# A gated mix of memory attention and a SwiGLU network on one core: attention visits by quads of heads, with shorter holds of PSUM banks

## The chip, the cores and the metric

The kernel runs on one core of one Trainium2 chip. Its engines are TensorE (PE, with PEld for its weight loads), VectorE (DVE), ScalarE (ACT), GpSimd (POOL) and SyncE (SP, which only issues transfers). The metric is the device time of one launch in microseconds. The kernel before took 1145.44 us as the median of three runs, which lay between 1144.23 and 1146.28.

## The reference

Input `x` has 2048 rows of 640 features. Two branches are computed from it and mixed by a gate per row.

```python
x = A_x                                     # [1, 2048, 640]
g = _sigmoid((x * gate_w).sum(-1, keepdims=True))
a = _A_ref(x, A_wq, A_wk, A_wv, A_wo, A_beta)
b = _B_ref(x, B_w1, B_w3, B_w2)             # (silu(x w1) * (x w3)) w2, 1728 hidden features
return g * a + (1 - g) * b

# _A_ref: 32 heads of 20 features, 4 segments of 512 rows
for s in range(N):
    qs, ks, vs = q[:, :, s], k[:, :, s], v[:, :, s]
    logits = jnp.einsum("bhqd,bhkd->bhqk", qs, ks) * scale + mask
    p = _softmax(logits, axis=-1)
    a_dot = jnp.einsum("bhqk,bhkd->bhqd", p, vs)
    pq = phi(qs)                            # where(t > 0, t + 1, exp(t))
    num = jnp.einsum("bhld,bhde->bhle", pq, M)
    den = jnp.einsum("bhld,bhd->bhl", pq, z)[..., None] + 1e-6
    o = g * num / den + (1.0 - g) * a_dot
    outs.append(o)
    pk = phi(ks)
    M = M + jnp.einsum("bhld,bhle->bhde", pk, vs)
    z = z + jnp.einsum("bhld->bhd", pk)
```

## The kernel before

**Numbers in two parts.** Each fp32 operand of the large products is held as a rounded part and a remainder, and a product is three matmuls (`PASSES`). `split` (L112) makes the parts: ScalarE casts (L113), GpSimd or VectorE subtracts (L114).

**Work beside attention.** The segments are handled as two groups, A (0 and 1) and B (2 and 3). For each group come the projections Q, K and V (`q_block`, `k_block`, `v_blocks`), the memory (`memory_turn`, `memory_write`), the reads of memory (`memory_read`, segments 1 to 3), the network (`ffn_up`, `ffn_down`) and the output projection (`oproj`). Each is a generator that yields after a few hundred nanoseconds of matmul work, with an estimate of it.

**Weights.** `w_load` (L155) issues the load of the next weight into one of two raw buffers, on SP. Items 0 and 1 are weights of Q, 2 to 6 those of V, 7 to 11 those of K, 12 the next of Q. `w_split` makes the two parts in one of six `W` tiles. A load waits until the raw buffer's last subtract is done.

**Attention.** A head has three units of logits. `s_unit` computes logits with queries as rows (L564), and VectorE takes the row maxima (L572, an addition of the mask with a running maximum). `max_rows` (L576) rounds the 8 columns of maxima of a pair of heads (L580), takes the remainder (L581) and turns 32 x 32 blocks (L584); transfers from GpSimd's queue (L587) put them as extra rows beside Q, so that `t_unit` (L589) gets transposed logits with the maximum already subtracted (L600). ScalarE takes exp into `P` (L605), GpSimd zeroes above the diagonal (L613). `pv_quad` (L618) multiplies P by V for four heads (L624); the values come in `vg` tiles for eight heads.

**The order.** TensorE's order is the program's. `attention` (L711) counts slots; a pair of heads has 20. At slots 5 and 15 a visit is made: the units of pair t's logits, of pair t-2's transposed logits, and every second pair P V. The loop at the end of `gated_mix` runs the other generators between visits, and before a visit steps up to four times until the group of matmuls in progress has reached `READY` (800). The other engines' orders come from a scheduler with estimated times, apart from what is pinned by `here` or `behind`.

**PSUM.** There are eight banks. `bank_tile` (L118) takes them in rotation. A projection or network group holds its bank out of the rotation until it is filled. `parts` (L274) empties a Q or K group: copy, exp, minimum with 1 (L282), remainder (L283), maximum with 0 plus the exp (L285).

```python
VISITS = {5: ((0, 1), (0,)), 15: ((2,), (1, 2))}      # slot: units of logits, units of P
P32 = sp.tile([P, 1280], F32, tag="P32", bufs=4)      # one per head
```

Of the kernel before, what the change touches and what calls it, by code (L numbers as in the profile page):

```python
# [27 lines left out]
RH, READY = 3 * DH, 800  # L28
NP, AGE = 4, 4
# [8 lines left out]
def gated_mix(ctx: ExitStack, tc: tile.TileContext, xT, wqk, wv, w13, w2, w2h, wo, beta, out):  # L38
# [15 lines left out]
    qk = [cp.tile([P, 2, L], FR, name=f"qk{i}") for i in range(NST)]  # L54
    gH = cp.tile([P, H], F32, name="gH")
# [10 lines left out]
    def constants():  # L66
# [4 lines left out]
        for i in range(2):  # L71
            nc.gpsimd.memset(nsT[i].bitcast(F32), 0.0)
# [45 lines left out]
    def bank_tile(name, hold=False):  # L118


        k = free.pop(0)
        ps = pp.tile([P, L], F32, tag=f"b{k}", name=name, bufs=1)
        if hold:
            held[k] = 0
        else:
            free.append(k)
        return ps

    def filled():

        (k, _), = held.items()
        held.clear()
        free.append(k)
# [19 lines left out]
    raws, clock = [], dict(step=0, oldest=0, next=0)  # L153

    def w_load():  # L155
        k = clock["next"]
        src, n = items[k]
        if k in EARLY:
            raw = sp.tile([P, 1280], F32, tag="P32", name=f"wr{k}", bufs=NP)
        else:  # L160
            raw = sp.tile([P, D + 2], F32, tag="wraw", name=f"wr{k}", bufs=NRAW)
        nc.sync.dma_start(raw[:, :n], src)
# [111 lines left out]
    def parts(name, ps, phi=None):  # L274
# [4 lines left out]
        if phi is not None:  # L279
            e = f_tile("phi_t")  # L280
            last["act"] = nc.scalar.activation(e, ps, AF.Exp)
            nc.vector.tensor_scalar(e, e, 1.0, None, op0=ALU.min)  # L282
        nc.vector.tensor_sub(s[:, 1], ps, s[:, 0].bitcast(F32))  # L283
        if phi is not None:
            nc.vector.scalar_tensor_tensor(phi, ps, 0.0, e, op0=ALU.max, op1=ALU.add)  # L285
# [19 lines left out]
    def q_block(c, mb, i, alloc, oldest=None):  # L305
        ps = bank_tile(f"q{c}_{mb}", True)
# [8 lines left out]
    def memory_read(c):  # L315
        pq = big.pop(("q", c))[:, :KB * L].rearrange("p (b n) -> p b n", b=KB)
        for qb in range(4):
            gm = ht_tile([P, D], F32, f"gm{c}_{qb}")
            for hf in range(2):
# [8 lines left out]
                for n, (b, a0, u0, u1) in enumerate(todo):  # L328
# [3 lines left out]
                                     start=n == 0, stop=n == len(todo) - 1, skip_group_check=True)  # L332
                r = sp.tile([P, 16], F32, tag="r16", name="nd_r")
# [9 lines left out]
    def v_blocks(c, iv, end):  # L343
# [7 lines left out]
        for lb in range(4):  # L351
# [5 lines left out]
            for hf in range(2):  # L357
                n0, n1 = (0, 320) if hf == 0 else (320, 642)
                ps = bank_tile(f"v{c}_{lb}_{hf}", True)
# [20 lines left out]
    def k_block(c, mb, i, prev):  # L380
# [3 lines left out]
        ps = bank_tile(f"k{c}_{mb}", True)  # L384
# [85 lines left out]
    def ffn_up(cs, j, idx, oldest=None):  # L470
        half = j == NF
        for c in cs:
            ws = [w_get(i, idx[0] if oldest is None else oldest) for i in idx]
            x = Xs[c]
            pg = bank_tile(f"g{c}_{j}", True)
# [5 lines left out]
            if not half:  # L481
# [5 lines left out]
                pu = bank_tile(f"u{c}_{j}", True)  # L487
# [3 lines left out]
            else:  # L491
# [5 lines left out]
                nc.gpsimd.tensor_sub(ht[64:, 0], t[:64], ht[:64, 0].bitcast(F32))  # L497
            yield 699

    def ffn_down(cs, js, idx, last=False):  # L500
        first = js[0] == 0
        w2s = [w_get(i, idx[0]) for i in idx]
        for c in cs:
            if first:
                accs[c] = slot(f"acc{c}")[:, :4 * D].rearrange("p (b d) -> p b d", b=4)
            for lb in range(4):
                for hf in range(2):
                    ps = bank_tile(f"f{c}_{js[0]}_{lb}_{hf}", True)
# [22 lines left out]
    def load_pair(p):  # L531
# [9 lines left out]
        if h % 8 == 0:  # L541
            v = sp.tile([P, 4, VG + 12], F32, tag="vg", name=f"vg{j}", bufs=NVG)
            nc.gpsimd.memset(v[:, :, VG:], 0.0)
            i = nc.sync.dma_start(v[:, :, :VG], vd[c][:, :, VE * h:VE * h + VG])
            if j < 8:
                here(i)
            bank["v"] = v
        m = sp.tile([P, 8], F32, tag="m", name=f"m{j}", bufs=4)
# [3 lines left out]
        pairs[p] = dict(t=t, m=m)  # L552
# [457 lines left out]
```

## Time and profile before

| | |
|---|---|
| Median of three runs | 1145.44 us |
| The profiled execution | 1145.62 us |
| Its span in the profile | 1143.9 us |
| Mean granted clock of TensorE | 0.997 |
| Busy: PE, DVE, POOL, ACT | 1125.0, 651.0, 558.7, 449.7 us |
| Bytes moved | 152.05 MB, mean 133 GB/s |

The largest groups of matmuls are those of the network (L251 `g` and `u`, 216.8 and 202.3 us; L514 `f`, 204.0 us). Of attention's groups, L564 and L624 have 76.3 and 75.5 us. VectorE's largest group is the row maxima, 250.8 us; GpSimd's is the subtract of weight parts, 197.6 us.

How to read it: a line of the timeline gives the start, the time, the engine and line, the operation with its tiles and shape, and in brackets how long the engine was idle before it and what ended that. A group of lines gives busy time and mean nanoseconds of one. A window gives its length and then each engine's busy time in it. An issue of a transfer (SPq, POOLq, ACTq) is not counted as busy.

### The profile page before, as it was taken

What the parts mean: (1) busy time and instruction counts of PE and PEld (TensorE: products, weight loads), DVE (VectorE), ACT (ScalarE), POOL (GpSimd) and SP (SyncE); (2) the same over time, 40 slices, a digit from 0 to 9 for tenths busy, and PEclk for the clock granted to TensorE, in tenths of its full rate; (3) what the DMA queues carried; (4) which work ended last, traced back from release to release, by engine and by line L of the source; (5) the groups of instructions that cost most, each with busy time, mean ns of one, the idle gap of its engine ahead of it and who ended that gap; (6) DMA issues with size and microseconds to landing.
All of it is one profiled execution on the core that took longest, in us unless ns stands there. A gap on an engine that the chain in (4) does not pass through costs nothing.

```text
span 1143.9 us, 19984 instructions
## 1 busy us (share of the span) xinstructions
PE 1125.0 (98%) x6953; PEld 904.9 (79%) x6953; DVE 651.0 (57%) x1987; ACT 449.7 (39%) x884; POOL 558.7 (49%) x811
## 2 busy tenths in 40 slices
PE   9989999999999999999999989999999999999998
PEld 6978877877877897878977766868778787877888
DVE  5033475555655653565345788775666776662534
ACT  5244234544343333253444534435543344344140
POOL 5053355555555346365354445664764457454150
PEclk9999999999999999999999999999999999999999
DMA  8275733324434225325386765363534324342112
GB/s 323 91 226 196 246 105 91 98 79 122 107 98 115 66 74 157 104 73 178 108 271 228 267 185 138 97 183 110 176 104 108 100 69 138 91 132 64 48 58 93
DMA packets 84725, 152.05 MB, mean 133 GB/s; under 512 B 19728, under 2 KB 29456, under 8 KB 84624
## 3 DMA queue, kind: packets, MB, share of 16 engines
q1 hardware_dynamic: 55632, 98.29, 26.2%
q0 software_dynamic: 22080, 38.58, 13.8%
q10 hardware_dynamic: 6912, 13.90, 3.3%
q8 instruction: 56, 0.92, 0.3%
q14 instruction: 45, 0.37, 0.1%
HBM read 95.25 MB, written 54.53 MB: 131 GB/s over the span
## 4 chain that ended last, share of the span: by engine, by line
PE 87%; issue 4%; DVE 3%; DMA 3%; POOL 1%; ACT 1%; SPq 0%; POOLq 0%; ACTq 0%; DVEq 0%
PE f L514 17%; PE g L251 17%; PE u L251 16%; PE o L624 6%; PE q L251 6%; PE s L564 5%; PE v L363 4%; PE k L251 4%; PE op L765 4%; PE t L600 3%; DMA wr<-in_wqk_dram 1%; PE pm L417 1%; PE nd L329 1%; DVE junk L572 1%; POOL W L114 1%
## 5 line engine op out<-in xcount | busy, mean ns | idle before, releaser
L572 DVE CUSTOM_DVE_ANT_0 junk<-s,mask 128x128 bf16<-128x128 f32 (+3 forms) x512 | 250.8, 490 | 153.9 <-PE s L564 117.5
L114 POOL TENSOR_TENSOR W<-wr,W 128x640 fp32r<-128x640 f32 (+1 forms) x126 | 197.6, 1574 | 253.6 <-ACT W L113 201.5
L605 ACT ACTIVATE P<-t 128x384 f32<-128x384 f32 (+1 forms) x384 | 174.7, 530 | 280.9 <-PE t L600 165.5
L251 PE MATMUL g<-X,W 128*128 128x512 f32 x840 | 216.8, 401 | 1.4 <-DVE ns L581 1.4
L514 PE MATMUL f<-W,ht 128*128 128x320 f32 x1312 | 204.0, 313 | 1.7 <-DVE m L572 1.2
L251 PE MATMUL u<-X,W 128*128 128x512 f32 x780 | 202.3, 401 | 0.0
L514 PEld LDWEIGHTS f<-W,ht 128*128 128x128 f32 x1312 | 194.5, 189 | 8.8 <-issue 2.6
L251 PEld LDWEIGHTS g<-X,W 128*128 128x128 f32 x840 | 153.4, 188 | 40.9 <-issue 7.2
L613 POOL TENSOR_SCALAR_AFFINE_SELECT P<-P 128x256 f32<-128x256 f32 x256 | 98.4, 416 | 159.4 <-ACT P L605 159.4
L251 PEld LDWEIGHTS u<-X,W 128*128 128x128 f32 x780 | 142.8, 188 | 36.7 <-issue 3.7
L113 ACT CAST W<-wr 128x640 fp32r<-128x640 f32 (+1 forms) x133 | 95.4, 728 | 96.1 <-PE u L251 20.2
L114 POOL TENSOR_TENSOR ht<-ft,ht 128x512 fp32r<-128x512 f32 x52 | 67.1, 1290 | 66.3 <-ACT ht L113 64.6
L522 DVE SCALAR_TENSOR_TENSOR acc<-f,cgate,acc 128x320 f32<-128x320 f32 x128 | 68.9, 546 | 42.3 <-PE f L514 41.8
L587 POOL DMA_DIRECT2D qk<-mr x128 | 72.6, 570 | 20.2 <-DVE mr L584 13.4
L624 PE MATMUL o<-P,vg 128*32 128x512 f32 (+3 forms) x1024 | 75.5, 435 | 2.2 <-DVE gm L337 1.6
L251 PE MATMUL q<-X,W 128*128 128x512 f32 x300 | 76.6, 407 | 0.9 <-DVE X L114 0.7
L540 POOL DMA_DIRECT2D qk<-qkd x128 | 70.4, 554 | 14.1 <-PE t L600 10.8
L251 PE MATMUL k<-X,W 128*128 128x512 f32 x300 | 77.2, 404 | 0.0
L564 PE MATMUL s<-qk 60*128 60x256 f32 (+2 forms) x512 | 76.3, 373 | 0.2 <-DVE oall L691 0.2
L483 DVE SCALAR_TENSOR_TENSOR fu<-ft,g 128x512 f32<-128x512 f32 x52 | 35.7, 686 | 70.9 <-ACT ft L482 70.6
L765 PE MATMUL op<-W,oT 128*128 128x320 f32 x480 | 74.3, 312 | 0.0
L765 PEld LDWEIGHTS op<-W,oT 128*128 128x128 f32 x480 | 71.1, 189 | 2.5 <-issue 1.5
(104 smaller groups left out, 1190.2 us busy)
## 6 DMA issues: line engine op xcount, KB each, us to landing
qk<-qkd POOLq DMA_DIRECT2D x128, 240.0 KB, 3.8
wr<-in_w_dram SPq DMA_DIRECT2D x80, 320.0 KB
qkd<-qs SPq DMA_DIRECT2D x20, 512.0 KB
qkd<-ks SPq DMA_DIRECT2D x20, 512.0 KB
od<-oq ACTq DMA_DIRECT2D x32, 256.0 KB
wr<-in_wqk_dram SPq DMA_DIRECT2D x21, 320.0 KB
wr<-in_wo_dram SPq DMA_DIRECT2D x20, 320.0 KB
vg<-vd SPq DMA_DIRECT2D x16, 336.0 KB
```

The source lines that it names most:

```text
L113: pin(nc.scalar.copy(dst[:, 0], src))
L114: (lo or nc.gpsimd.tensor_sub)(dst[:, 1], src, dst[:, 0].bitcast(F32))
L251: nc.tensor.matmul(ps, w[:, a, kb * P:(kb + 1) * P], x[:, b, kb, :], start=n == 0, stop=n == 14)
L514: nc.tensor.matmul(ps[:, :320], a, b, start=n == 0, stop=n == len(ms) - 1)
L540: here(nc.gpsimd.dma_start(t[64 * i:64 * i + RH], qkd[c][RH * (h + i):RH * (h + i + 1)]))
L564: nc.tensor.matmul(ps[i][:, o:o + n], q[:, qb * P:(qb + 1) * P], k[:, :n], start=qb != 1, stop=qb != 0, skip_group_check=True)
L572: nc.vector.tensor_tensor_reduce(out=junk[:, :n], in0=ps[i][:, o:o + n], in1=mask[:, L - n:], scale=1.0, scalar=-3.0e38, op0=ALU.add, op1= ...
L587: after(5, lambda d=dst, a=a: here(nc.gpsimd.dma_start(d, mr[8 * a:8 * a + 8])))
L605: last["exp"] = nc.scalar.activation(P32[:, o:o + n], ps[i][:, b:b + n], AF.Exp, scale=SCALE)
L613: nc.gpsimd.affine_select(d, d, pattern=[[0, 2], [1, P]], base=0, channel_multiplier=-1, compare_op=ALU.is_ge, fill=0.0)
L624: nc.tensor.matmul(ps[32 * i:32 * i + 32, kb * P:], u["v"][:, kb], u["P32"][:, o:o + n], start=kb == 0, stop=kb == 3, skip_group_check=True)
L765: nc.tensor.matmul(ps[:, :320], oT[0][:, qb % 2, a, kb * P:(kb + 1) * P], ws[kb][:, b, 320 * hf:320 * hf + 320], start=n == 0, stop=n == 14)
```

## The change

It regroups attention by quads of heads and moves work that empties PSUM. The program works through a quad in 40 slots with four visits, of 5 + 3 + 4 + 4 units in another order; P times V is the first thing in its visit; row maxima of two pairs are turned together; the two heads of a pair share one P tile; masks are applied in three instructions for a pair, some of them earlier.

```diff
-RH, READY = 3 * DH, 800
-NP, AGE = 4, 4
+RH, LEAD = 3 * DH, 20
+NP, AGE = 2, 4
...
-    VISITS = {5: ((0, 1), (0,)), 15: ((2,), (1, 2))}
+    VISITS = {5: (((0, 0), (0, 1)), ((0, 0),)), 15: (((0, 2), (1, 0)), ((0, 1),)),
+              25: (((1, 1), (1, 2)), ((0, 2),)), 35: ((), ((1, 0), (1, 1), (1, 2)))}
...
+        for m in range(-1, NQUAD + 2):
+            for n in range(40):
...
+                    if n == 5 and 0 <= m - 2 < NQUAD:
+                        pv_quad(2 * m - 4)
+                    if 0 <= m < NQUAD:
+                        for i, x in us:
+                            s_unit(2 * m + i, x)
+                    if 0 <= m - 1 < NQUAD:
+                        for i, x in ut:
+                            t_unit(2 * m - 2 + i, x)
+                    if n == 25 and 0 <= m < NQUAD:
+                        max_rows(2 * m)
+                elif n in ((22, 32) if m < 0 else (27, 37)) and m + 1 < NQUAD:
+                    load_pair(2 * (m + 1) + (n > 27))
...
-        ns = nsT[p % 2]
-        nc.vector.tensor_copy(ns[:, :8], m)
-        nc.vector.tensor_sub(ns[:, 8:16], m, ns[:, :8].bitcast(F32))
+        ns = nsT[p // 2 % 2]
+        nc.vector.tensor_copy(ns[:, :16], m)
+        nc.vector.tensor_sub(ns[:, 16:], m, ns[:, :16].bitcast(F32))
...
-        for a in range(2):
-            dst = pairs[p]["t"][RH + a:RH + a + 65:64, 0].rearrange("h (b n) -> h b n", n=P)
-            after(5, lambda d=dst, a=a: here(nc.gpsimd.dma_start(d, mr[8 * a:8 * a + 8])))
+        for k in range(2):
+            for a in range(2):
+                dst = pairs[p + k]["t"][RH + a:RH + a + 65:64, 0].rearrange("h (b n) -> h b n", n=P)
+                r = 16 * a + 8 * k
+                after(5 + 8 * k, lambda d=dst, r=r: here(nc.gpsimd.dma_start(d, mr[r:r + 8])))
...
-        for i in range(2):
-            P32 = hd[i]["P32"]
-            d0 = P32[:, :1024].rearrange("p (a b) -> p a b", a=2)[:, :, :P]
-            d1 = P32[:, 896:1152].rearrange("p (a b) -> p a b", a=2)
+        for a, n in (((0, 1),), (), ((512, 1), (896, 2)))[t]:
+            d = u["P"][:, :, a:a + n * P].rearrange("p h (a b) -> p h a b", b=P)
```

Outside attention: the closing work on Q and K reads PSUM in another order, a memory read is copied out of PSUM by ScalarE before VectorE works on it, the weights 7 to 12 are loaded from GpSimd's queue, and each kind of group has its own hold (1300 for projections and `ffn_up`, 800 for V and the output projection, 700 for `ffn_down`) before a visit may come. When no group is in progress the loop goes on stepping as before.

```diff
-        nc.sync.dma_start(raw[:, :n], src)
+        (nc.gpsimd if 7 <= k < 13 else nc.sync).dma_start(raw[:, :n], src)
...
             last["act"] = nc.scalar.activation(e, ps, AF.Exp)
-            nc.vector.tensor_scalar(e, e, 1.0, None, op0=ALU.min)
+            nc.vector.tensor_scalar(phi, ps, 0.0, None, op0=ALU.max)
         nc.vector.tensor_sub(s[:, 1], ps, s[:, 0].bitcast(F32))
         if phi is not None:
-            nc.vector.scalar_tensor_tensor(phi, ps, 0.0, e, op0=ALU.max, op1=ALU.add)
+            nc.vector.scalar_tensor_tensor(phi, e, 1.0, phi, op0=ALU.min, op1=ALU.add)
...
+                ns = f_tile("nds")[:, :16 * VE].rearrange("p (h e) -> p h e", e=VE)
+                nc.scalar.copy(ns, nd)
+                nd = ns
                 r = sp.tile([P, 16], F32, tag="r16", name="nd_r")
...
-                if max(held.values(), default=0) >= READY:
+                if max(held.values(), default=-1) >= 0:
...
-            v = sp.tile([P, 4, VG + 12], F32, tag="vg", name=f"vg{j}", bufs=NVG)
-            nc.gpsimd.memset(v[:, :, VG:], 0.0)
-            i = nc.sync.dma_start(v[:, :, :VG], vd[c][:, :, VE * h:VE * h + VG])
-            if j < 8:
-                here(i)
+            bank["v"] = v = vg[j // 8 % NVG]
+            here(nc.sync.dma_start(v[:, :, :VG], vd[c][:, :, VE * h:VE * h + VG]))
...
-                nc.gpsimd.tensor_sub(ht[64:, 0], t[:64], ht[:64, 0].bitcast(F32))
+                nc.vector.tensor_sub(ht[64:, 0], t[:64], ht[:64, 0].bitcast(F32))
```

Smaller edits: the two `vg` tiles are fixed and their padding is cleared once; the early weights 2 to 5 come in pairs in P's tiles; the loads of memory reads (`load_memory`) are spread among the network's steps instead of issued in a row; the lead before the first pair is 20 slots (24 before), and the second stretch of work ends one head later.

More of the change, by code (lines that the diff above doesn't have):

```diff
@@ L123, in bank_tile @@
         if hold:
-            held[k] = 0
+            held[k] = -hold
         else:
@@ L129, in filled @@
     def filled():
-        (k, _), = held.items()
+        free.extend(held)
         held.clear()
-        free.append(k)
     def ht_tile(shape, dt, name):
```

94 lines of the change are left out of this document (38 added, 56 removed).

## The prediction

> **What bounds the kernel now.** I read the page's first two parts, then who waits for whom on PE, then 20 us windows, then the timeline around each wait.
>
> ```profile
> span 1143.9 us, 19984 instructions
> PE 1125.0 (98%) x6953; PEld 904.9 (79%) x6953; DVE 651.0 (57%) x1987; ACT 449.7 (39%) x884; POOL 558.7 (49%) x811
> ...
> PE pm L417 <- ACT pkn L404: 3.0, 1, 3.0
> PE o L624 <- DVE gm L337: 1.6, 2, 0.9
> PE t L600 <- DVE pq L285: 1.6, 1, 1.6
> ...
> PE f L514 <- DVE m L572: 1.2, 1, 1.2
> ```
>
> TensorE is busy 98% of the span. The change issues the same matmuls (every family of L251, L363, L514, L564, L600, L624, L765 in the same number and shape), so only the 2% can move: 1143.9 - 1125.0 = 18.9 us, and some slow stretches inside the busy time. Of the named waits one is for ScalarE (a copy of K's transposed block), the others are for VectorE, which empties PSUM too late. The windows tell where:
>
> ```profile
> 72.00:74.00 2.00, 0.48 (x3) 0.04 (x1) 0.00 (x0) 0.71 (x2) 0.00 (x0) 1.00 0.81 277
> 74.00:76.00 2.00, 0.48 (x2) 0.48 (x3) 0.98 (x2) 1.47 (x4) 1.91 (x2) 0.77 0.30 113
> 76.00:78.00 2.00, 2.00 (x9) 1.98 (x9) 1.10 (x2) 0.11 (x1) 0.43 (x2) 0.50 0.99 280
> ...
> 640.00:660.00 20.00, 18.29 (x116) 12.66 (x115) 15.96 (x49) 10.10 (x21) 10.47 (x18) 1.00 0.88 297
> 660.00:680.00 20.00, 17.33 (x107) 12.89 (x108) 15.74 (x56) 5.98 (x12) 5.41 (x10) 0.91 0.61 182
> ...
> 740.00:760.00 20.00, 18.12 (x125) 13.32 (x124) 13.69 (x49) 8.26 (x15) 14.95 (x20) 1.00 0.72 212
> 760.00:780.00 20.00, 18.78 (x130) 14.33 (x129) 15.76 (x58) 7.30 (x15) 9.93 (x18) 1.00 0.46 138
> 780.00:800.00 20.00, 20.00 (x157) 17.27 (x156) 7.96 (x34) 10.46 (x22) 7.09 (x12) 1.00 0.36 94
> ```
>
> The columns after the window's length are PE, PEld, DVE, ACT, POOL busy, the granted clock, DMA share, GB/s. Two places hold most of the loss. At 72 to 76 us PE is short of 2 x 1.52 = 3.0 us, and the clock falls to 0.50 just after: about 1 us more in 76 to 78. In the four windows between 640 and 780, PE is short of 1.71 + 2.67 + 1.88 + 1.22 = 7.5 us, with a clock of 0.91 in one (0.09 x 20 = 1.8 us). There VectorE is busy some 75 to 80%, against 40% in the full window after.
>
> **The K weights (part one).**
>
> ```profile
> 62.70 3.09 POOL L114 TENSOR_TENSOR W<-wr,W 128x640 fp32r<-128x640 f32 x2 [3.06 <-DMA wr<-in_wqk_dram]
> ...
> 66.10 0.41 SPq L162 DMA_DIRECT2D wr<-in_wqk_dram  x1
> ...
> 73.28 0.72 ACT L113 CAST W<-wr 128x640 fp32r<-128x640 f32 x1 [4.40 <-DMA wr<-in_wqk_dram]
> ...
> 74.88 0.59 ACT L404 COPY pkn<-pkt 128x512 f32<-128x512 f32 x1
> ...
> 75.52 2.33 PE L417 MATMUL pm<-V,pkn 128*128 128x147 f32 x8 [3.04 <-ACT pkn L404]
> ```
>
> ScalarE stands 4.40 us before the cast of a weight that isn't needed yet; queued behind it are the evacuation of K, the exp and the copy `pkn` that PE wants. The load took 73.28 - 66.10 = 7.2 us on SP's queue, among the K stores. The change issues items 7 to 12 from GpSimd. Item 13, the late one, stays on SP, but with fewer loads before it. In the changed order of ScalarE the casts of 12 and 13 come after `pkn`, ahead of the next evacuation. Against it: two raw buffers serve the stream, and GpSimd issues loads 10 and 11 only after both subtracts before them, load 12 likewise; one subtract is 3.09 / 2 = 1.55 us, so each pair is that much later. If item 13 lands at 73.3 + 1.55 = 74.9, five ScalarE operations of 0.6 us follow, 77.9; PE, unstalled, wants the next `pkn` some 19 matmuls after 72.5, near 77.3. So 0 to 0.6 us stays. Value -3.0; bounds -4.0 (wait and slow clock gone) and +3.0 (a wait as long again).
>
> [...]
>
> **VectorE and PSUM between 640 and 780 (part two).**
>
> ```profile
> 658.01 1.76 DVE L336 TENSOR_TENSOR nd_r<-nd_r,gH 128x16 f32<-128x16 f32 x1
> ...
> 658.17 1.56 POOL L114 TENSOR_TENSOR W<-wr,W 128x640 fp32r<-128x640 f32 x1
> ...
> 659.70 0.68 DVE L285 SCALAR_TENSOR_TENSOR pq<-q,phi_t 128x512 f32<-128x512 f32 x1
> ...
> 660.43 0.49 PE L600 MATMUL t<-qk 62*128 62x512 f32 x1 [1.56 <-DVE pq L285]
> ...
> 669.49 1.93 DVE L282 TENSOR_SCALAR phi_t<-phi_t 128x512 f32<-128x512 f32 x1
> ```
>
> A 16-column multiply lasts 1.76 us exactly while GpSimd subtracts a weight; behind it waits the operation that frees Q's bank, and PE loses 1.56 us. The usual costs of VectorE's and ScalarE's groups:
>
> ```profile
> L572 DVE CUSTOM_DVE_ANT_0 junk<-s,mask 128x512 bf16<-128x512 f32 x128 | 88.3, 690 | 71.9 <-PE s L564 63.6 <-PE f L514 0.5
> L572 DVE CUSTOM_DVE_ANT_0 junk<-s,mask 128x384 bf16<-128x384 f32 x128 | 71.1, 556 | 14.9
> ...
> L584 DVE STREAM_TRANSPOSE mr<-ns 32x32 f32<-32x32 f32 x256 | 51.2, 200 | 4.5
> ...
> L580 DVE CAST ns<-m 128x8 fp32r<-128x8 f32 x64 | 23.4, 365 | 1.8
> L581 DVE TENSOR_TENSOR ns<-m,ns 128x8 fp32r<-128x8 f32 x64 | 18.5, 290 | 1.8
> ...
> L282 DVE TENSOR_SCALAR phi_t<-phi_t 128x512 f32<-128x512 f32 x30 | 15.4, 514 | 71.4 <-ACT phi_t L281 71.3
> ...
> L337 DVE TENSOR_TENSOR gm<-nd,nd_r 128x320 f32<-128x320 f32 x24 | 11.7, 489 | 0.6
> ...
> L371 ACT COPY V<-v 128x320 f32<-128x320 f32 x24 | 10.3, 428 | 33.7 <-PE v L363 33.7
> ```
>
> Turning maxima by quads halves the counts of L580, L581, L584: (51.2 + 23.4 + 18.5) / 2 = 46.5 us of VectorE saved, 1.45 per quad; 16 columns instead of 8 I price as nothing (0 to 0.1 us). In `parts` the bank was held until min, subtract and the closing sum had run after the exp; now max and subtract alone read it, and the closing sum reads SBUF. VectorE's work there stays near 514 + 680 + 680 ns (the max from PSUM between 0.43 and 0.68), but the bank comes free about 0.5 + 0.7 us earlier. A memory read's bank is freed by one ScalarE copy (between L371's 0.43 and 0.59 of `pkn`, 24 times = 10 to 14 us on an engine at 39%) instead of by four VectorE operations, of which the last alone has 0.49 and one can last 1.76. P's exps also stop waiting for P V of the same visit. All of this acts on the waits of 9.3 us. I take two thirds: -6.0; bounds -9.3 and 0. The visits now fall in mid group of `f` (hold 700, where 800 was never reached), worth -0.7 of the 1.2 us wait `f <- m` (0 to -1.2).
>
> [...]
>
> **New waits (part three).**
>
> ```profile
> 246.09 0.50 PE L564 MATMUL s<-qk 60*128 60x512 f32 x2
> ...
> 248.44 3.63 PE L251 MATMUL g<-X,W 128*128 128x512 f32 x15
> ...
> 254.24 2.36 PE L624 MATMUL o<-P,vg 128*32 128x512 f32 x32
> ...
> 246.81 1.64 ACT L605 ACTIVATE P<-t 128x384 f32<-128x384 f32 x4 [2.11 <-PE t L600]
> ...
> 247.43 1.50 POOL L613 TENSOR_SCALAR_AFFINE_SELECT P<-P 128x256 f32<-128x256 f32 x4 [3.03 <-ACT P L605]
> ...
> 253.61 1.14 POOL L587 DMA_DIRECT2D qk<-mr  x2
> ...
> qk<-mr POOLq DMA_DIRECT2D x128, 4.0 KB, 3.2
> ...
> L329 PE MATMUL nd<-Ms,pq 128*128 128x147 f32 x96 | 17.2, 303 | 0.3 <-DVE gm L337 0.3
> ```
>
> Masks: exps and selects end 2.8 us after the visit at 246.09, P V starts 8.1 after. In the new order these four exps and two of 512 columns (0.6 us, as the copy `pkn`) belong to one visit, so 4.0 us, and 18 to 24 matmuls of 3.63 / 15 = 0.24 us plus the visit's 0.8 lie between, 5 to 6.5 us: covered by 1 to 2 us. If that cover goes, PE waits. Row maxima: the first pair of a quad was 30 slots ahead of its P logits and is 20 now. From the last logits to the first P logits I count 11 to 14 us of matmuls in the dense stretches (23 quads). Need: four maxima of the two units, 2 x 0.56 + 2 x 0.69, the turning 0.37 + 0.29 + 4 x 0.2, so 4.0 us and with gaps 5; issue 0.6 and landing 3.2, so 9 us: covered. At quad 0 only 21 projection matmuls, 9 of memory reads and 0.6 us of logits lie between: 21 x 0.24 + 9 x 17.2 / 96 + 0.6 = 7.3 us, no P V yet, so it comes 1.7 short. Value +2.0 (0 to +4). In the quoted case GpSimd issued the maxima 7.5 us after the logits; with the second issue and 3.2, 11.3, the cover is at its end. For such cases, late pair loads (18 slots instead of 27) and P V I take +1.5 in all (0 to +23, one us in each of 23 quads). P V ahead of the visit changes one switch of tile shape per quad: 0, bounds +-0.1 x 32 = 3.2. SP takes the `vg` loads in program order, each behind a P V two quads old; memory loads are spread instead of in a burst; the first weights share larger tiles: 0 each, within the bounds of the pair loads. Sixteen memsets less, three selects for four and four subtracts moved from GpSimd to VectorE (0.7 us each) are hidden by engines at half load.
>
> **Sum.** -3.0 - 6.0 - 0.7 + 2.0 + 1.5 = -6.2. The profiled execution took 1145.62 us (span 1143.9 and 1.7 around it), 0.2 above the median of 1145.44; so 1145.4 - 6.2 = 1139.2.
>
> **The rivals.** [...] (2) Slower: the maxima of each quad's first pair. Place: the first P logits of a quad. Price: what landing exceeds the 11 to 14 us. It decides from a landing of 12 us on; at 0.6 us over 23 quads 14 us, less 6 gained: 1153. For it: the 7.5 us issue above. Against it: usually the need is 9. (3) GpSimd's queue does harm: later K weights bring a wait of 3 us and a slow clock at K, and blocked multiplies leave 640 to 780 as it is: 1145.4 + 3.0 + 1.5 = 1150. [...]
>
> **How the numbers follow.** Forecast 0.62 (its own range 1131 to 1143), rival 1 0.14, rival 2 0.14, rival 3 0.10. I count as no change what lies within 0.2%, 2.3 us, about what three runs can tell. Faster: 0.62 and a little of rival 1, 0.63; same 0.13; slower 0.24. The range takes most of the bounds below (-4.0 - 9.3 - 1.2 with 1 us of new waits gives 1132, less the switch 1129) and rivals 1 and 3 and the lower half of 2 above: 1129 to 1152.
>
> **What would show it.** PE's wait `pm <- pkn` near 72 us gone and no 0.50 clock behind it; the four windows of 640 to 780 within 1 us of full; rows of the transposes at 128 instead of 256 in count, each 200 ns; a wait of 1 to 3 us of the first P logits near 150 us, and few later. Wrong it is if P logits wait on the maxima's DMA in quad after quad, if P V waits for GpSimd's selects, or if K waits for weights loaded by GpSimd.

## The result, and the profile after

The changed kernel took 1148.51 us (median of 20 runs, 1146.31 to 1151.66), the kernel before, beside it on the same chip, 1145.95 us (20 runs, 1141.53 to 1150.05). The ratio is 1.0021, with a 95% interval of 1.0011 to 1.0031: slightly slower, where 6.2 us less was forecast. The profiled execution took 1149.21 us. First its page, then who waits for whom on PE (total, times, longest):

```profile
span 1147.3 us, 19590 instructions
...
PE 1127.9 (98%) x6953; PEld 908.8 (79%) x6953; DVE 635.4 (55%) x1799; ACT 462.5 (40%) x908; POOL 552.8 (48%) x733
```

```profile
PE t L603 <- DVE fu L489: 5.0, 4, 1.8
PE t L603 <- DVE acc L528: 3.2, 1, 3.2
PE s L567 <- DVE nd_r L342: 1.4, 1, 1.4
PE t L603 <- DMA qk<-mr: 1.3, 1, 1.3
```

VectorE has less to do (635.4 against 651.0 us) and K's wait is gone, yet PE's idle time is the same: 1147.3 - 1127.9 = 19.4 us against 18.9. The waits have moved to the P logits (`t`, the transposed logits), and they are again for VectorE. The windows (PE, PEld, DVE, ACT, POOL busy, granted clock, DMA share, GB/s) say where, first of after, then two of before:

```profile
72.00:74.00 2.00, 2.00 (x14) 1.74 (x13) 0.30 (x1) 1.14 (x3) 1.68 (x2) 1.00 0.56 206
74.00:76.00 2.00, 2.00 (x12) 1.74 (x11) 0.68 (x2) 1.09 (x2) 1.93 (x3) 1.00 0.17 44
...
500.00:520.00 20.00, 16.78 (x84) 14.69 (x83) 17.61 (x31) 9.96 (x20) 13.22 (x17) 0.83 0.31 80
640.00:660.00 20.00, 18.68 (x115) 13.19 (x114) 13.93 (x44) 9.45 (x20) 8.31 (x14) 1.00 0.78 256
660.00:680.00 20.00, 19.16 (x132) 14.54 (x132) 18.35 (x62) 10.96 (x23) 9.72 (x15) 1.00 0.73 228
740.00:760.00 20.00, 17.63 (x113) 13.80 (x106) 13.59 (x44) 8.33 (x16) 13.16 (x16) 0.91 0.67 190
760.00:780.00 20.00, 18.94 (x134) 14.20 (x132) 16.19 (x55) 10.22 (x21) 10.17 (x14) 1.00 0.42 124
780.00:800.00 20.00, 19.64 (x144) 16.87 (x144) 8.34 (x31) 10.21 (x21) 8.24 (x14) 0.91 0.48 127
900.00:920.00 20.00, 17.90 (x116) 11.90 (x114) 13.92 (x35) 7.47 (x14) 10.25 (x16) 1.00 0.37 103
```

```profile
500.00:520.00 20.00, 18.79 (x113) 16.74 (x112) 17.09 (x33) 8.18 (x15) 15.91 (x17) 1.00 0.45 141
900.00:920.00 20.00, 20.00 (x130) 14.00 (x129) 16.67 (x43) 9.66 (x19) 11.10 (x15) 1.00 0.40 121
```

- K: 72 to 76 is full. With the slow clock behind it, this place gained 3.0 + 0.23 x 2 + 0.50 x 2 = 4.5 us.
- 640 to 780: the four windows are short of 1.32 + 0.84 + 2.37 + 1.06 = 5.6 us, 1.9 less than before. But beside the clock of 0.91 in one of the four, as before, there is now a second in the window just behind them (780 to 800), which costs 0.09 x 20 = 1.8 us. Nothing is left.
- 500 to 520: 2.0 us more idle time and a clock of 0.83, together 2.0 + 0.17 x 20 = 5.4 us lost. 900 to 920: 2.1 us lost.

The slow clock lasts 13.65 us in three stretches (from 512.45, 754.80 and 782.10 us) against 6.83 us before. At the clock of 0.50 that was granted in each of them, this is 3.4 us, as much as the spans differ. The timeline at two of the three places (start, length, engine, line, [idle time before and what ended it]):

```profile
507.38 1.16 POOL L592 DMA_DIRECT2D qk<-mr  x2 [1.42 <-DVE mr L587]
...
508.18 4.95 DVE L115 TENSOR_TENSOR X<-xr,X 128x512 fp32r<-128x512 f32 x1
508.56 1.58 POOL L115 TENSOR_TENSOR W<-wr,W 128x642 fp32r<-128x642 f32 x1
510.09 1.27 POOL L115 TENSOR_TENSOR X<-xr,X 128x512 fp32r<-128x512 f32 x1
511.31 1.26 POOL L115 TENSOR_TENSOR ht<-ft,ht 128x512 fp32r<-128x512 f32 x1
513.05 3.29 DVE L528 SCALAR_TENSOR_TENSOR acc<-f,cgate,acc 128x320 f32<-128x320 f32 x7
...
513.65 3.08 PE L603 MATMUL t<-qk 62*128 62x512 f32 x8 [3.22 <-DVE acc L528]
...
752.42 1.53 POOL L115 TENSOR_TENSOR W<-wr,W 128x640 fp32r<-128x640 f32 x1 [0.91 <-ACT W L114]
...
752.70 1.28 DVE L340 TENSOR_SCALAR nd_r<-nds 128x16 f32<-128x16 f32 x1 [2.62 <-ACT nds L337]
...
754.18 0.63 DVE L489 SCALAR_TENSOR_TENSOR fu<-ft,g 128x512 f32<-128x512 f32 x1
...
754.86 0.79 PE L603 MATMUL t<-qk 62*128 62x256 f32 x3 [1.77 <-DVE fu L489]
```

A subtraction of X that usually takes 0.68 us on VectorE lasts 4.95, until GpSimd is through with three subtractions in a row. Seven `acc` stand in line behind it, and the visit of eight matmuls of P logits wants their banks. At 752 it is the addition of a memory read, which now reads the copy `nds` in SBUF, and `fu` behind it. The groups of VectorE (count, busy us, mean ns), after and then before:

```profile
L587 DVE STREAM_TRANSPOSE mr<-ns 32x32 f32<-32x32 f32 x128 | 25.6, 200 | 2.2
...
L343 DVE TENSOR_TENSOR gm<-nds,nd_r 128x320 f32<-128x320 f32 x24 | 16.4, 682 | 0.9 <-DMA gd<-gm 0.3
L287 DVE SCALAR_TENSOR_TENSOR pq<-phi_t,pq 128x512 f32<-128x512 f32 x15 | 14.4, 960 | 0.0
...
L287 DVE SCALAR_TENSOR_TENSOR pk<-phi_t,pk 128x512 f32<-128x512 f32 x15 | 13.2, 879 | 0.0
L584 DVE TENSOR_TENSOR ns<-m,ns 128x16 fp32r<-128x16 f32 x32 | 12.8, 401 | 0.7
...
L340 DVE TENSOR_SCALAR nd_r<-nds 128x16 f32<-128x16 f32 x24 | 11.7, 487 | 5.6 <-ACT nds L337 5.6
L583 DVE CAST ns<-m 128x16 fp32r<-128x16 f32 x32 | 11.0, 344 | 0.6
```

```profile
L285 DVE SCALAR_TENSOR_TENSOR pq<-q,phi_t 128x512 f32<-128x512 f32 x15 | 10.2, 681 | 0.0
L285 DVE SCALAR_TENSOR_TENSOR pk<-k,phi_t 128x512 f32<-128x512 f32 x15 | 10.2, 679 | 0.0
...
L334 DVE TENSOR_SCALAR nd_r<-nd 128x16 f32<-128x16 f32 x24 | 3.9, 163 | 2.8 <-PE nd L329 2.5
```

The addition, the multiply and the closing sums (now a minimum and an addition in one) are 0.2 to 0.3 us longer in the mean once their operands lie in SBUF instead of PSUM: 163 to 487, 489 to 682, 680 to 960 and 879 ns. Counting what each VectorE operation lasts over the lower quartile of its group, from 0.3 us on, 22 operations were held for 21 us before, and 42 for 48 us after. I call these the holds. A stall, below, is the time by which a visit lasts longer than the median of the visits with the same matmuls in its kernel.

### The profile page after: what moved, and what is told of

The parts are those of the page before. It is cut to its first block, busy times and chain, and to the rows that moved or that the text cites. A ratio compares the mean times of both kernels' runs of the same rounds, so it can differ in the third digit from the quotient of the medians.

```text
span 1147.3 us, 19590 instructions
## 1 busy us (share of the span) xinstructions
PE 1127.9 (98%) x6953; PEld 908.8 (79%) x6953; DVE 635.4 (55%) x1799; ACT 462.5 (40%) x908; POOL 552.8 (48%) x733
## 4 chain that ended last, share of the span: by engine, by line
PE 89%; DVE 5%; issue 3%; DMA 2%; POOL 1%; ACT 0%; SPq 0%; POOLq 0%; ACTq 0%; DVEq 0%
PE f L520 17%; PE g L253 16%; PE u L253 15%; PE o L620 6%; PE v L369 6%; PE k L253 6%; PE q L253 5%; PE s L567 5%; PE op L763 4%; PE t L603 4%; DVE junk L575 2%; PE pm L423 1%; PE nd L331 1%; PE pkt L408 1%; POOL W L115 1%
## 5 line engine op out<-in xcount | busy, mean ns | idle before, releaser
L610 POOL TENSOR_SCALAR_AFFINE_SELECT P<-P 128x256 f32<-128x256 f32 (+1 forms) x192 | 96.5, 507 | 239.2 <-ACT P L607 238.3
L520 PE MATMUL f<-W,ht 128*128 128x320 f32 x1312 | 206.7, 315 | 0.3 <-POOL W L115 0.3
L520 PEld LDWEIGHTS f<-W,ht 128*128 128x128 f32 x1312 | 197.1, 191 | 6.9 <-issue 3.4
L528 DVE SCALAR_TENSOR_TENSOR acc<-f,cgate,acc 128x320 f32<-128x320 f32 x128 | 69.2, 546 | 40.8 <-PE f L520 40.2
L603 PE MATMUL t<-qk 62*128 62x256 f32 (+2 forms) x512 | 71.6, 344 | 10.3 <-DVE fu L489 5.0
L620 PE MATMUL o<-P,vg 128*32 128x256 f32 (+3 forms) x1024 | 76.1, 436 | 0.0
L369 PE MATMUL v<-W,X 128*128 128x320 f32 (+1 forms) x480 | 72.0, 311 | 0.0
L369 PEld LDWEIGHTS v<-W,X 128*128 128x128 f32 x480 | 71.1, 189 | 0.6 <-issue 0.2
```

The lines of the kernel that those rows point to most:

```text
L369: nc.tensor.matmul(ps[:, :n1 - n0], x[:, a, kb, lb * P:(lb + 1) * P], wvt[kb][:, b, n0:n1], start=n == 0, stop=n == 14)
L520: nc.tensor.matmul(ps[:, :320], a, b, start=n == 0, stop=n == len(ms) - 1)
L603: nc.tensor.matmul(ps[i][:, o:o + L - q0], k[:, kb * P:(kb + 1) * P], q[:, q0:], start=kb != 2, stop=kb != 3, skip_group_check=True)
L610: nc.gpsimd.affine_select(d, d, pattern=[[0, 2], [0, n], [1, P]], base=0, channel_multiplier=-1, compare_op=ALU.is_ge, fill=0.0)
L620: nc.tensor.matmul(ps[32 * i:32 * i + 32, kb * P:], heads[2 * p + i]["v"][:, kb], pairs[p + i // 2]["P"][:, i % 2, o:o + n], start=kb == 0 ...
```

## The experiments

Two theories stood against each other. Holds: the new way of emptying PSUM exposes VectorE's operations to GpSimd, and PE pays. Order: quads make a long line on VectorE (four maxima and the turning at slot 25) just ahead of a visit at slot 35 whose three units are all P logits, eight matmuls. (Each of the four visits of a quad has three units with two banks each, and one has P V besides; it isn't 5 + 3 + 4 + 4 units, as stands ahead of the prediction. The largest visit of the kernel before has six matmuls of P logits.) Ratios are to the kernel before, run beside each, with 95% intervals.

| run | us | ratio | holds, us |
|---|---|---|---|
| changed kernel | 1148.5 | 1.0021 (1.0011 to 1.0031) | 48 |
| a_reads_psum | 1148.1 | 1.0006 (0.9993 to 1.0020) | 38 |
| b_x_gpsimd | 1147.5 | 0.9997 (0.9984 to 1.0011) | 46 |
| c_k_sync | 1149.6 | 1.0017 (1.0004 to 1.0030) | 52 |
| d_before_k_pv | 1140.3 | 0.9934 (0.9915 to 0.9953) | 21 |
| e_before_k_pv_emptying | 1142.1 | 0.9958 (0.9940 to 0.9977) | 34 |
| f_quads_old_emptying | 1149.1 | 1.0012 (0.9994 to 1.0030) | 32 |
| g_w_vector | 1150.0 | 1.0012 (0.9997 to 1.0027) | 12 |
| h_f_whole | 1149.1 | 1.0018 (1.0003 to 1.0033) | 57 |
| i_before_k | 1140.9 | 0.9956 (0.9939 to 0.9973) | 22 |
| j_before_pv | 1143.5 | 0.9977 (0.9962 to 0.9993) | 17 |
| k_after_pairs | 1143.4 | 0.9975 (0.9963 to 0.9988) | 45 |
| l_quads_even | 1135.0 | 0.9908 (0.9885 to 0.9930) | 32 |
| m_lag | 1143.0 | 0.9975 (0.9962 to 0.9988) | 48 |
| n_even_old_emptying | 1135.0 | 0.9898 (0.9884 to 0.9911) | 22 |
| o_before_lag | 1147.3 | 1.0003 (0.9987 to 1.0019) | 23 |
| p_before_k_pv_lag | 1145.3 | 0.9980 (0.9964 to 0.9997) | 20 |
| q_even_pace7 | 1148.3 | 1.0019 (1.0004 to 1.0034) | 24 |
| r_after_pace7 | 1158.2 | 1.0094 (1.0074 to 1.0115) | 52 |

### The parts that gain: K's weights, and P times V first

Into the kernel before went the one, the other, or both:

```diff
-        nc.sync.dma_start(raw[:, :n], src)
+        (nc.gpsimd if 7 <= k < 13 else nc.sync).dma_start(raw[:, :n], src)
...
                     yield "visit"
+                    if n == 5 and 0 <= t - 3 < NPAIR and t % 2 == 0:
+                        pv_quad(2 * (t - 4))
...
-                    if n == 5 and 0 <= t - 3 < NPAIR and t % 2 == 0:
-                        pv_quad(2 * (t - 4))
```

> The kernel before with two parts of the change alone: the six weight loads from GpSimd's queue, and P times V ahead of the units of its visit instead of behind. If both gains read from the two traces are real and stand alone (about 5 us at K with its slow clock, and 0.04 to 0.13 us in each of 32 visits with P times V, some 3 us), and the rest of the change is what costs, it takes 1137 to 1140. If P times V first gains nothing by itself (as the prediction priced it), 1140 to 1142; if the gain at K needs the earlier release of K's bank, 1142 to 1146.

> The kernel before with one part of the change alone: K's six weights loaded by GpSimd. The wait of 3.0 us at 72 to 75 us and the half clock behind it (3.4 us) go, as in the kernel with both parts (1140.3 us, ratio 0.9934). If the two parts add up as the traces say (about 5 at K, about 3 in the visits), 3.5 to 5.5 us less than the kernel before, ratio 0.995 to 0.997. If P times V is all of it, ratio 0.998 to 1.001.

> The kernel before with the other part alone: P times V ahead of the units of its visit. By the traces a visit with it takes 3.23 us instead of 3.36 behind a projection and 3.27 behind a network group: 2 to 4 us less in 32 visits, ratio 0.9965 to 0.998; the stall at 72 us stays. If the prediction's price of nothing is right and K is all of the gain, ratio 0.999 to 1.001.

Together 0.9934; alone 0.9956 (5.0 us) and 0.9977 (2.6 us), which multiply to 0.9933. At this pace the two add up; j's gain is barely clear of its noise, and at the pace of o and p below both together are worth 2.6 us. d came to the border of two of its ranges; i and j lie where a gain by each part alone was forecast. Without K's part the wait at 72 us stays, as j's list of waits has it:

```profile
PE pm L417 <- ACT pkn L404: 3.5, 1, 3.5
```

P V's part isn't seen in its visits. From the start of the matmul ahead of a visit with P V to the start of the one behind it takes 3.454 us in the median before and 3.455 us in j and in the changed kernel (some 30 visits each). So the saving of 0.04 to 0.13 us per visit, on which the expectations of d and j rest, isn't there, and where j's 2.6 us come from is not shown. In the changed kernel the loads were put back:

```diff
-        (nc.gpsimd if 7 <= k < 13 else nc.sync).dma_start(raw[:, :n], src)
+        nc.sync.dma_start(raw[:, :n], src)
```

> The changed kernel with the six weight loads back on SP's queue. If the prediction's part one is right as it stands, the wait of the memory product on the normalized copy of K near 72 us comes back (about 3 us) with about 3.4 us of half clock behind it, and the time rises by 4 to 6 us over the changed kernel, to 1152 to 1155. If the stall went because of another part of the change (the bank released earlier in the emptying of K), there is no stall near 72 us, and the time stays within 1.5 us of the changed kernel.

Ratio 1.0017 against 1.0021: no difference, as its second forecast had it. c's windows show no wait near 72 us:

```profile
72.00:74.00 2.00, 2.00 (x12) 1.51 (x11) 1.44 (x3) 1.00 (x3) 1.44 (x2) 1.00 0.61 231
74.00:76.00 2.00, 2.00 (x14) 1.69 (x13) 0.44 (x1) 1.23 (x3) 1.14 (x3) 1.00 0.95 267
```

So something else in the change also suffices to take this wait away; what, was not tried alone. GpSimd's loads are enough, not needed.

### The new emptying of PSUM

From the changed kernel the copy of the memory reads was taken (a), and with it the maximum (f); the two were put on top of d (e); and taken from the evenly spread quads below (n).

```diff
-                ns = f_tile("nds")[:, :16 * VE].rearrange("p (h e) -> p h e", e=VE)
-                nc.scalar.copy(ns, nd)
-                nd = ns
...
-            nc.vector.tensor_scalar(phi, ps, 0.0, None, op0=ALU.max)
+            nc.vector.tensor_scalar(e, e, 1.0, None, op0=ALU.min)
...
-            nc.vector.scalar_tensor_tensor(phi, e, 1.0, phi, op0=ALU.min, op1=ALU.add)
+            nc.vector.scalar_tensor_tensor(phi, ps, 0.0, e, op0=ALU.max, op1=ALU.add)
```

> The changed kernel with one part undone: a memory read is again worked on by VectorE straight from PSUM, without the ScalarE copy into SBUF (L337). Theory 1 (holds): VectorE operations whose operands all lie in SBUF are held while GpSimd subtracts two SBUF tiles; the copy made the addition, the multiply by the gate and the last multiply of each memory read such operations (held 12 times, 15 us over their usual length in the changed kernel, against 3 times and 3.3 us before). Then the addition (24 rows) and the last multiply go back to their usual 0.17 and 0.49 us in every instance, the stalls at 752 (3.3 us) and 778 us (1.8 us) shrink to below 1.5 us each, the half clock behind them goes, and the time falls by 3 to 7 us against the changed kernel, to 1142 to 1146. Theory 2 (banks): it is the order of the units that makes VectorE late, and the copy helps; then the stalls there stay or grow, and the time is that of the changed kernel or up to 4 us more.

> The kernel before with K's weights loaded by GpSimd, P times V ahead of its visit (these two together took 1140.3 us, ratio 0.9934 to the kernel before), and now also both new ways of emptying PSUM: the maximum in place of the minimum, and the ScalarE copy of each memory read. The visits by pairs and the maxima by pairs stay. Theory 1 (holds): the emptying puts operands of four more VectorE operations in SBUF only, GpSimd holds them, and PE pays: the lengths above the usual of VectorE's operations rise from 21 to over 30 us, and the time goes to 1143 to 1147. Theory 2 (order by quads): the emptying is harmless or helps by up to the 6 us that the prediction gave it: 1135 to 1140, and the stalls at 655, 662 and 747 us (2.2, 1.4 and 2.8 us with those two parts alone) shrink by half.

> The other half: the changed kernel with both ways of emptying PSUM as they were before (the minimum in place of the maximum, the memory reads from PSUM without a copy); quads, early P times V, K's weights by GpSimd and all else as changed. Theory 1 (holds by the emptying): the lengths above the usual fall from 48 to below 30 us, and the time falls by 5 us or more against the changed kernel, to 1140 to 1144. Theory 2 (order by quads): the stalls of the visits of eight transposed logits at 513 and 903 us stay (5.5 and 2.5 us) and the time is within 3 us of the changed kernel, 1146 to 1151.

> The evenly spread quads with PSUM emptied as before the change: the minimum in place of the maximum, memory reads by VectorE from PSUM. If the two new ways of emptying cost because GpSimd holds their operations (as 1140.3 against 1142.1 us on the order of before hinted, and 1149.1 against 1148.5 on the changed one did not), the lengths above the usual fall from 32 to below 25 us and it takes 1131 to 1134, ratio 0.987 to 0.990. If the emptying is worth what the prediction gave it (6 us, less where the order is easier), 1137 to 1141, ratio 0.992 to 0.995. Within 1.5 us of 1135 it is neither.

The lengths do what the theory of holds says. In f, with PSUM operands again:

```profile
L340 DVE TENSOR_TENSOR gm<-nd,nd_r 128x320 f32<-128x320 f32 x24 | 11.8, 490 | 0.6
L287 DVE SCALAR_TENSOR_TENSOR pk<-k,phi_t 128x512 f32<-128x512 f32 x15 | 10.2, 680 | 0.0
```

The time doesn't follow them. Undoing the emptying changes the ratio by -0.0009 (f) and -0.0010 (n), undoing the copy alone by -0.0015 (a), and adding the emptying by +0.0024 (e), each inside its noise. In a the stalls at 752 and 778 us shrank from 3.3 to 1.7 and from 1.8 to 0 us, but others of 0.9 and 1.8 us came at 662 and 772, and those at 513 and 900 stayed at 5.5 and 2.4. The emptying is worth nothing, or costs up to 3 us; the 6 us forecast for part two can't come from it on any of the three orders. Neither theory was met in full: a and f took the time of the second, but f's holds fell to 32 us and not below 30, e came between its two forecasts, and n to neither.

### Holds, and the interrupted groups

Three more edits of the changed kernel: X's remainders by GpSimd alone (b), the weights' remainders by VectorE alone (g), and the hold of `f` back at 800 (h).

```diff
-            split(Xs[c][:, :, kb, :], xraw[c][kb], lo=nc.vector.tensor_sub if kb % 2 else None, pin=here)
+            split(Xs[c][:, :, kb, :], xraw[c][kb], lo=None, pin=here)
...
-        split(w[:, :, :n], raw[:, :n], lo=nc.vector.tensor_sub if k < 7 else None, pin=behind(after))
+        split(w[:, :, :n], raw[:, :n], lo=nc.vector.tensor_sub, pin=behind(after))
...
-                    ps = bank_tile(f"f{c}_{js[0]}_{lb}_{hf}", 700)
+                    ps = bank_tile(f"f{c}_{js[0]}_{lb}_{hf}", 800)
```

> The changed kernel, with all ten remainders of segments 2 and 3 of X taken by GpSimd instead of four by VectorE. In the changed kernel one of VectorE's four lasts 4.95 us at 508, across three GpSimd subtracts in a row, then the network's accumulations stand in line behind it, and the visit of eight transposed logits at 513.65 starts 3.4 us late and costs 5.5 us over its usual time, with 6.8 us of half clock behind. Theory 1 (holds): without the held subtract that stall falls below 1 us and no half clock follows near 512; 5 to 8 us less than the changed kernel, 1141 to 1144. Theory 2 (order): the visit comes in the middle of a network group and asks for six banks at once, whatever VectorE subtracts; then the stall stays above 3 us and the time within 2 us of the changed kernel.

> The changed kernel with the remainders of all weights taken by VectorE (0.83 us each) instead of GpSimd (1.56 us), so that GpSimd can hold VectorE with these subtracts nowhere; they end 22 of the 48 us of holds in the changed kernel. Theory 1 (holds): stalls at 752, 778 and 903 us fall below 1 us each; the stall at 513 us falls as well, since the held remainder of X there stands first behind a weight's subtract; the time falls by 4 to 8 us. Theory 2 (VectorE's line is too long at these visits, whatever holds it): about 100 remainders of 0.83 us more on VectorE make the stalls longer, and the time rises by 3 us or more.

> The changed kernel with the hold of a network group `f` at 800 again instead of 700, so that a visit waits for the end of a group of nine matmuls and doesn't come after five. The stalls at 513 (5.5 us) and 778 us (1.8 us) and the slow clock behind each stand in such interrupted groups. If the interruption is the cause (a bank less is free while the group is held), both stalls fall below 1 us, and the time falls by 4 to 9 us. If VectorE is late for its own reasons, the stall moves to the next visit and the time stays within 2 us of the changed kernel.

b: 2.7 us less by the ratio, between the two forecasts. The stall of 5.5 us became 1.4 and, behind it, a wait of 2.0 us of `f` for GpSimd's remainder of `ht`, and the slow clock stayed. g removed three quarters of the holds. The stalls at 513, 778 and 903 us fell from 5.5, 1.8 and 2.5 to 2.5, 0.7 and 0.9 us, that at 752 stayed at 3.2, and a new one of 3.1 us came at 645, with new waits of 1.3 us at 74 (for ScalarE's `pkn`) and 1.8 at 579 (for VectorE's `pk`). So the holds have a part in three of those stalls, but taking them away by lengthening VectorE's line gains nothing: 1.0012, which neither theory forecast. h: 1.0018, the stall of 5.5 us stands as it was: the interrupted groups are not its cause.

### The order of the units

k goes back to pairs, with all else as changed; l keeps the turning by quads and spreads the units evenly; m is l's control, with only the pace (`LAG`) altered. The core: the slots of the changed kernel, k's and then l's, and the pace of l and m:

```diff
-    VISITS = {5: (((0, 0), (0, 1)), ((0, 0),)), 15: (((0, 2), (1, 0)), ((0, 1),)),
-              25: (((1, 1), (1, 2)), ((0, 2),)), 35: ((), ((1, 0), (1, 1), (1, 2)))}
+    VISITS = {5: (((0, 0), (0, 1)), ((0, 0),)), 15: (((0, 2),), ((0, 1), (0, 2))),
+              25: (((1, 0), (1, 1)), ((1, 0),)), 35: (((1, 2),), ((1, 1), (1, 2)))}
...
+    VISITS = {5: (((0, 0), (0, 1)), ((-1, 2),)), 15: (((0, 2),), ((0, 0), (0, 1))),
+              25: (((1, 0), (1, 1)), ((0, 2),)), 35: (((1, 2),), ((1, 0), (1, 1)))}
...
-LAG = 5
+LAG = 6
```

In k `max_rows` follows at slots 15 and 35 for one pair each; in l it follows at slot 35, P V comes at slot 15, and the second pair is loaded at slot 7.

> The changed kernel with the logits in the order of before: per pair two units and one, with their P logits two pairs behind, maxima rounded and turned by pairs in eight columns; all else as changed (emptying, holds, K's weights, P times V first, selects joined). If the order by quads is what costs (theory 2): there are no visits of eight transposed logits, the stalls at 513 and 903 us (5.5 and 2.5 us) fall below 2 and 1 us, and it takes 1140 to 1144, as the kernel before with emptying, K and P times V (1142.1). If the smaller edits (holds, joined selects, spread loads of the memory, the network's half block on VectorE) cost, it stays at 1146 to 1150.

> The changed kernel with the maxima still turned by quads, but the units spread evenly: four visits with 4 and 2, 2 and 4, 4 and 2, 2 and 4 groups of banks of logits and transposed logits, the turning at slot 35, the first P logits 20 slots behind it, the last unit of a quad one visit into the next and P times V at slot 15. If the visit of eight transposed logits behind the longest line on VectorE (four maxima and the turning) is what costs, the stalls at 513 and 903 us fall below 2 and 1 us, and the time falls by 4 to 9 us against the changed kernel, to 1139 to 1145. If turning by quads itself costs (its operations held by GpSimd, the maxima late), it stays within 3 us of the changed kernel, 1146 to 1151.

> A control for the evenly spread quads (1135.0 us, ratio 0.9908 to the kernel before): the changed kernel in its own order, with nothing altered but the constant that sets how many slots the other work is stretched over (LAG 6 instead of 5), as that kernel needed it. If the even spread is the cause, this one keeps the visits of eight transposed logits and stays within 4 us of the changed kernel, ratio 0.999 to 1.004, with t visits among its longest stalls. If the looser pace is the cause, ratio 0.990 to 0.994.

k takes 5 us less than the changed kernel, as forecast; l 13 us less, more than either forecast; and m, which keeps the order, also takes 5 us less, between its two. By the traces the pace alone moved the work of 500 to 520 and of 900 to 920 us past the visits that stalled. Its longest stalls are at other visits (3.2 us at 746, 2.8 at 779). Against this control the even spread is worth 0.9908 / 0.9975 = 0.993, some 8 us. About 5 of them are seen in the visits: their stalls over 0.1 us add up to 15.4 us in m, 8.8 of it in the visits of eight P logits, and to 10.3 us in l, where no visit has more than four. l's windows at the two places:

```profile
500.00:520.00 20.00, 20.00 (x123) 17.94 (x122) 17.86 (x40) 11.19 (x21) 15.59 (x17) 1.00 0.38 118
...
900.00:920.00 20.00, 19.94 (x136) 14.98 (x135) 13.98 (x39) 10.12 (x19) 10.49 (x13) 1.00 0.44 114
```

### The pace

The kernel before and d at `LAG` 6 (o, p); n and the changed kernel at `LAG` 7 (q, r). The edit is that constant alone.

> The kernel before with the looser pace alone (LAG 6), as the control for what that pace is worth on the old order. On the changed kernel it was worth 5 us: the stall at 513 us and its slow clock went, since X's held remainder no longer falls ahead of a visit. If the pace is a gain of its own, ratio 0.995 to 0.997. If on the changed kernel it only moved an unlucky coincidence away, the kernel before has no such stall to lose: ratio 0.998 to 1.003.

> The kernel before with K's weights by GpSimd, P times V first and the looser pace: the two parts that gained, in the order by pairs, at the pace of the evenly spread quads (1135.0 us, 0.9898 with the old emptying). If the even quads owe their time to 46 us less of VectorE's work, this one stays at 1139 to 1142, ratio 0.993 to 0.996. If K's weights, P times V and the pace are all of it, 1134 to 1137, ratio 0.988 to 0.991.

> The evenly spread quads with the old emptying (1135.0 us, ratio 0.9898) at a third pace, LAG 7. If the even spread is good because VectorE's line ahead of each visit is shorter, wherever the other work falls, ratio 0.988 to 0.993. If its time was a lucky placement, as 1140.3 us was for the kernel before with K's weights and P times V (0.9934 at LAG 5, 0.998 at LAG 6), 0.994 to 0.999.

> The changed kernel at LAG 7 (1.0021 at LAG 5, 0.9975 at LAG 6). If its own order with visits of eight transposed logits is worse than the even spread at every pace, ratio 0.996 to 1.003, and the t visits hold the longest stalls again. If only the coincidence at 513 us was costly, it comes to 0.992 to 0.996.

The pace is no gain of its own: 1.0003 on the kernel before, as forecast. On the others it moves the time either way: d lost 5 us with it (0.9934 to 0.9980), the changed kernel gained 5 and then lost 14 (1.0021, 0.9975, 1.0094 at 5, 6 and 7), the even spread lost 14 (0.9898 to 1.0019). p, q and r lay outside both of their forecasts. r's worst places are 500 to 520 and a new one:

```profile
500.00:520.00 20.00, 16.77 (x91) 13.45 (x94) 16.91 (x16) 8.27 (x17) 13.65 (x15) 0.89 0.30 76
...
760.00:780.00 20.00, 14.16 (x81) 9.70 (x80) 9.27 (x28) 6.69 (x15) 10.46 (x15) 0.83 0.54 178
```

In r the visits of eight P logits hold stalls of only 1.0 us in all. The longest waits are others: at 516.5 `f` stands 3.2 us for GpSimd's remainder of `ht`, and at 773.8 a memory read stands behind ScalarE, which waits for a weight.

```profile
772.54 0.72 ACT L114 CAST W<-wr 128x640 fp32r<-128x640 f32 x1 [9.45 <-DMA wr<-in_w_dram]
773.80 1.70 PE L331 MATMUL nd<-Ms,pq 128*128 128x147 f32 x6 [4.08 <-ACT oq L624]
```

The even spread is ahead of the changed kernel's order by 0.7% at 6 (l against m) and by 0.7% at 7 (q against r, of which the emptying may be 0.1). At 7 this isn't the doing of the eight P logits, though, and at 5 the even spread wasn't run.

## Why the prediction was wrong

| term of the sum | forecast, us | measured, us |
|---|---|---|
| K's weights | -3.0 (-4.0 to +3.0) | -4.5 in the windows; -5.0 alone (i) |
| VectorE and PSUM, 640 to 780 | -6.0 (-9.3 to 0) | -1.9 idle, +1.8 slow clock; the emptying alone +1 to +3, inside the noise (a, e, f, n) |
| the hold of 700 at `f <- m` | -0.7 (-1.2 to 0) | 0 (h); the place lost 5.4 instead |
| maxima of quad 0 late | +2.0 (0 to +4) | no wait for the transfer there; 1.1 at 156 us behind a held L340 |
| other new waits | +1.5 (0 to +23) | 5.4 at 500 to 520, 2.1 at 900 to 920 |
| P V ahead of the visit | 0 (-3.2 to +3.2) | -2.6 alone (j), not seen in its visits |

**The step that failed** is "All of this acts on the waits of 9.3 us. I take two thirds: -6.0". The mechanism was half right: the waits `o <- gm` and `t <- pq` are gone, the bank is free earlier. But, as I read the rows, those waits were for the place in VectorE's line, not for the bank's own operations. With the bank freed early, PE waits for `fu` and `acc` in the same line, and there the line didn't get shorter: with the holds VectorE is busy 17.6 us of 500 to 520 (17.1 before) and 18.4 us of 660 to 680 (15.7 before). The holds had no price in the sum, though two long rows stood in the trace of before: the multiply of 1.76 us at 658.01 and the minimum of 1.93 us at 669.49, beside subtractions of GpSimd of 1.56 and 1.57 us. Of VectorE's operations that start while GpSimd subtracts, at least 0.1 us before its end, those of five groups with all operands in SBUF were lengthened in 27 of 30 cases (L340 3 of 3, L343 3 of 3, L584 6 of 6, L583 5 of 6, L287 10 of 12), those of four groups with one operand in PSUM in none (L489 0 of 6, L495 0 of 5, L528 0 of 12, L285 before 0 of 13). L340, L583 and the minimum have a single SBUF input, the others of these five groups and the multiply have two. Not every operation on SBUF is lengthened: of the transposes L587 none of 11, of the reciprocals before none of 3.

**The second miss** is a size: "other new waits +1.5". The bound of +23 was taken from 23 quads with one us each. What came was two places, with 7.5 us together, at visits of eight P logits, with the slow clock behind the larger. I had priced the visits' order by what data each needs (maxima, selects, loads), and all of these were in time, as forecast: one wait of 1.3 us for the maxima, none for the loads, 0.5 us for the selects. Who stands in line ahead of the operations that free each visit's banks, I hadn't listed. No run shows the 0.1 us per quad in the bounds for P V; its visits took 3.454 us in the median before and 3.455 after.

**Right** were K (more than forecast, though in the changed kernel c shows that the loads are not what does it) and the work saved: L583, L584 and L587 take 49.4 us instead of 93.1, 43.7 less where 46.5 was forecast; VectorE's total fell by only 16 us. Of the rivals, the third came nearest in time (1150), but not by its reason: K wasn't harmed, and the waits of 640 to 780 moved rather than stayed.

**What stays open.** The loss of 2.6 us isn't a property of the order by quads alone. K and P V gain 7.6 us in the order by pairs; at this pace the rest of the change costs 10. Undone one after the other, the order gives back 5.3 of them (changed kernel to k), the smaller edits 1.9 (k to e: holds, joined selects, spread loads, four subtractions on VectorE) and the emptying 2.8 (e to d). The last two are within the noise, and of the smaller edits only the hold of `f` was tried alone (h). The pace alone gives back as much as the order (m). At `LAG` 6 the changed kernel and p, with the two gaining parts alone, are equal (0.9975 and 0.9980). I found no tally (holds, idle time, line on VectorE) that says ahead of a run what a pace brings.

## What to carry to other kernels

Before a PSUM bank is freed by a copy to SBUF, look at whether the engine that reads next is itself late: here it was, the copy gained nothing (1.0021 with it, 1.0006 without, a), and the operations that moved from PSUM to SBUF came under GpSimd's holds (48 us in the changed kernel, 32 with the old emptying, f). An order of work is priced by what each step wants freed and by the line ahead of the freeing operation. An order with bursts (one unit of P logits at each of three visits, three at the fourth) took 8 us more than an even spread of the same units at one pace, with 5 us of it in longer visits. A change that shifts all the other work should be run at two or three paces, since the same order moved by 14 us with a constant that does nothing else; the best kernel here, the evenly spread quads with the old emptying at `LAG` 6 with 1135.0 us (0.9898, 0.9884 to 0.9911), is partly such a find.

## What the runs showed of the hardware that I had not expected

**Slow clock after short stalls.** The clock of 0.50 comes in whole stretches of 3.413 us (two of them in a row from 512.45 us after) on a grid of that period (from 75.10 and 662.19 us before: 172 periods apart; from 512.45, 754.80 and 782.10 us after: 71 and 8 apart). In the profiles of 18 of the 20 kernels (d and n have no slow stretch ahead of their last microseconds) I counted the time without a matmul in each period at full speed. With 2.0 us or more the next period was slow 12 times of 12, with 1.7 to 2.0 us 10 of 15, with 1.3 to 1.7 us 10 of 27, below that, the first 10 us left out, 3 times in over 5800. So 1.3 to 2.0 us without a matmul, some 40 to 60% of a period, were enough 20 times of 42. By an estimate from these counts a stall of 2 us costs 1.7 us more (half of 3.413), or nothing, by how it falls on the grid. Runs of one kernel differ in their clock: k's twelve runs lie between 1140.5 us at a mean clock of 0.999 and 1145.0 at 0.994.

**One hold across several subtractions.** The X at 508.18 began during the issue of `qk <- mr`, 0.4 us ahead of GpSimd's first subtraction, and ended 0.56 us after the third. In r an X of VectorE at 509.64 lasts 7.38 us, across five. Whether the issue of a transfer holds VectorE by itself is not shown.
